# Attention's q, k and v products as pairs of 64-row matmuls with two partial sums each

## The chip, the cores and the metric

The kernel runs on one core of one Trainium2 chip. The metric is the device time of one execution in microseconds (us). A core has the engines TensorE (PE, with its weight loads shown apart as PEld), VectorE (DVE), ScalarE (ACT) and GpSimd (POOL), and a queue on SyncE (SP) that issues all DMA transfers of this kernel in order.

## The reference, cut to what matters

```python
S, D, H, F = 2048, 576, 32, 4608             # Dh = 18, float32 throughout
def reference(A_x, A_wqkv, A_wo, B_x, B_w_gate, B_w_up, B_w_down):
    x = A_x
    xn = layernorm(x)
    q, k, v = heads(xn @ A_wqkv)              # [2048, 576] x [576, 1728]
    s = concat(softmax(q @ k.T * Dh**-0.5) @ v) @ A_wo
    g = silu((gelu(xn @ B_w_gate) * (xn @ B_w_up)) @ B_w_down)
    return x + s * g
```

Every float32 product is built from parts that TensorE's faster float32 format holds exactly: each operand is split into a high part (rounded to that format) and a low part (the rest), and high x high, low x high and high x low are added up.

## The kernel before, in words

The kernel has three stages. A prologue normalises x, transposes it and makes q, k and v. A long middle runs the gate, up and down products of the feed-forward network on TensorE between the attention's score, exponential and value work. An epilogue projects the attention output and multiplies it with the gate. The change touches the prologue alone.

**Blocks and products.** The prologue works on four blocks of 512 tokens (`NB`). `load_x` loads four x tiles of 128 tokens, `norm` computes their statistics on VectorE (`bn_stats`, `bn_aggr`, a few tiny steps) and normalises them, and `transposes` transposes them on TensorE into five PSUM banks; four banks hold the first 512 of the 576 columns, and the fifth holds the last 64 twice, since `norm` copies columns 512 to 576 once more behind the row. `split_t` makes the high part (ACT) and the low part (VectorE) of each bank: `xth`, `xtl`, and one tile `xtr` whose rows 0 to 63 are high and 64 to 127 low. `store_xt` writes them to DRAM (`xhs`) for the feed-forward stage.

For each block, `project` makes nine products of 128 q or k columns by 512 tokens (in the order `ORDER`), and `values_of` eight products of 128 tokens by 288 v columns. `mm_terms` (L174) issues each as 14 matmuls over all 128 rows into one PSUM bank `po`: four chunks each of high x high, low x high and high x low, and two for the last 64 rows. After a q/k product ACT copies the high part `t1` out of PSUM (L290), VectorE subtracts for the low part `t2` (L291), and SP stores both in `qk` (L293). After a v product ACT copies it to one of eight `vn` tiles (L300), and SP stores that in `vs` (L301).

**What sets the order.** TensorE's instructions stand as the program writes them; the other queues are ordered by a scheduler, except where `keep_in_program_order` or a dependence added by hand (`after`) says otherwise. The transposes of the next block are written after the nine q/k products and before the eight v products. In the first block the weights come in as well: `load_qk` and `load_wv` load them to the five `rawp` buffers, GpSimd splits the q/k weights (`split_qk`, L106 and L108), ACT and VectorE the v weights and the 64 rest rows (L116, L117). SP also copies eight pieces of zeros to `zq` there (L376).

**PSUM.** The prologue has eight banks: five for transposes (`pt`) and three for products (`po`). `t1` and `t2` have three buffers each.

**Pairs elsewhere.** The gate and up products (L413) and most down products (L465) are already written as pairs: one matmul over rows 0 to 63 and one over rows 64 to 127, each into a bank of its own.

Of the kernel before, what the change touches and what calls it, by code (L numbers as in the profile page):

```python
# [8 lines left out]
F32 = mybir.dt.float32  # L9
F32R = mybir.dt.float32r  # L10
AF = mybir.ActivationFunctionType
ALU = mybir.AluOpType
# [42 lines left out]
def f(ap):  # L55
    return ap.bitcast(F32)
# [13 lines left out]
def kernel(ctx: ExitStack, tc: tile.TileContext, x, wqkv, wo, w_gate, w_up, w_down, out):  # L70
    nc = tc.nc
# [8 lines left out]
    qk = dram.tile([2, 2 * D, S], F32, name="qk")  # L80
    vs = dram.tile([S, H, DH + 1], F32, name="vs")
# [54 lines left out]
    def load_xd(b, key=None):  # L136
# [11 lines left out]
        return xd  # L148


    TERMS = [(0, k, 0) for k in range(KT)] + [(1, k, 0) for k in range(KT)] + [(0, k, 1) for k in range(KT)] \
        + [(0, KT, 2), (1, KT, 2)]

    FIRST_TERMS = sorted(TERMS[:2 * KT], key=lambda t: 2 * t[1] + 3 * t[0]) + TERMS[2 * KT:]


    with tc.tile_pool(name="pro", bufs=1) as pro, tc.tile_pool(name="pps", bufs=1, space=PSUM) as pps:
# [13 lines left out]
            keep(nc.sync.dma_start(raw, wqkv[0:R0, c0:c0 + n].rearrange("(k p) n -> p k n", p=P)))  # L171
            return raw

        def mm_terms(o, w, cols, xt, toks, swap=False, terms=TERMS):  # L174

            for i, (wp, k, xp) in enumerate(terms):
                xx = xt[xp][:, k, toks] if xp < 2 else xt[2][:, toks]
                ww = w[wp][:, k, cols] if k < KT else w[2 + wp]
                st, m = (xx, ww) if swap else (ww, xx)
                nc.tensor.matmul(o, st, m, start=(i == 0), stop=(i == len(terms) - 1))  # L180

        def tmp2(name):
            return pro.tile([P, TB], F32R, name=name, tag=name, bufs=3)

        def split_t(pt, k, xt):

            if k < KT:
                nc.scalar.activation(xt[0][:, k, :], pt, AF.Copy)
                nc.vector.tensor_tensor(xt[1][:, k, :], pt, f(xt[0])[:, k, :], op=ALU.subtract)
            else:  # L190
                nc.scalar.activation(xt[2], pt, AF.Copy)
                nc.vector.tensor_tensor(xt[2][HR:P, :], pt[HR:P], f(xt[2])[HR:P, :], op=ALU.subtract)

        def load_x(b):
            keep = tc.keep_in_program_order if b == 1 else lambda i: i
            xr = []
            for j in range(4):
                xx = pro.tile([P, D + HR], F32, name="xx", bufs=4)
                keep(nc.sync.dma_start(xx[:, 0:D], x[b * TB + j * P:b * TB + (j + 1) * P, :]))
                xr.append(xx)  # L200
            return xr
# [25 lines left out]

        def warm(n):

            o = pps.tile([P, TB], F32, name="po", bufs=3)  # L230
            for i in range(n):
                nc.tensor.transpose(o[:, 0:P], ident, ident)

        def transposes(b, xr):
            xt = XT[b % 2]
            pts = [pps.tile([P, TB], F32, name="pt", bufs=KT + 1) for k in range(KT + 1)]
            for j in range(4):
                if b == 0 and j == 0:
                    warm(46)
                for k in range(KT + 1):  # L240
                    nc.tensor.transpose(pts[k][:, j * P:(j + 1) * P], xr[j][:, k * P:(k + 1) * P], ident)  # L241
            for k in range(KT + 1):
                split_t(pts[k], k, xt)
            return xt

        def store_xt(b, xt):
            keep = tc.keep_in_program_order if b == 0 else lambda i: i
            for i in range(2):
# [1 line left out]
                keep(nc.sync.dma_start(xhs[b][i, R0:D, :], f(xt[2])[HR * i:HR * i + HR, :]))  # L250

        XT = [(pro.tile([P, KT, TB], F32R, name=f"xth{i}"), pro.tile([P, KT, TB], F32R, name=f"xtl{i}"),
               pro.tile([P, TB], F32R, name=f"xtr{i}")) for i in range(2)]
# [15 lines left out]
        def split_qk(t, raw):  # L269
            hi, lo = (pro.tile([P, KT, P], F32R, name=f"q{m}{t}") for m in "hl")  # L270
            first = split(hi, lo, raw)
            put_qk(t, hi, lo)
            return first
# [10 lines left out]
            WV[c] = hi, lo, VR[0][:, cc], VR[1][:, cc]  # L284

        def project(b, t, xt):
            o = pps.tile([P, TB], F32, name="po", bufs=3)
            mm_terms(o, WQK[t], slice(0, P), xt, all_t, terms=FIRST_TERMS if b == 0 and t == ORDER[0] else TERMS)
            hi, lo = tmp2("t1"), tmp2("t2")
            nc.scalar.activation(hi, o, AF.Copy)  # L290
            nc.vector.tensor_tensor(lo, o, f(hi), op=ALU.subtract)  # L291
            for i, a in enumerate((hi, lo)):
                nc.sync.dma_start(qk[i, t * P:(t + 1) * P, b * TB:(b + 1) * TB], f(a))  # L293

        def values_of(b, j, c, xt):
            t = b * 4 + j
            o = pps.tile([P, TB], F32, name="po", bufs=3)
            mm_terms(o[:, 0:D // 2], WV[c], slice(0, D // 2), xt, slice(j * P, (j + 1) * P), True)
            v = VN[2 * j + c]
            nc.scalar.activation(v[:, :, 1:DH + 1], o[:, 0:D // 2].rearrange("p (h d) -> p h d", d=DH), AF.Copy)  # L300
            nc.sync.dma_start(vs[t * P:(t + 1) * P, c * H // 2:(c + 1) * H // 2, :], v)  # L301

        def split_wo(k):
            n = min(P, D - k * P)
# [12 lines left out]
        t = ORDER[0]  # L317
# [21 lines left out]
        lo = nc.gpsimd.tensor_tensor(qlo, raw, f(qhi), op=ALU.subtract)  # L339
# [4 lines left out]
        xt = transposes(0, xr)  # L344
        for c0 in (slice((t + 1) * P, 2 * D), slice(0, t * P)):
            split_av(QR[0][:, c0], QR[1][:, c0], raw_r[:, c0], tc.keep_in_program_order)
        for b in range(NB):
            for n, t in enumerate(ORDER):
                if n == (2 if b == 0 else 0) and b + 1 < NB:
                    xr = load_x(b + 1)  # L350
                if b == 0 and ahead_qk:
                    first = split_qk(*ahead_qk.pop(0))
                    if n < 3:
                        after(first, last)
                    if n + 4 < NQT:
                        ahead_qk.append(load_qk(ORDER[n + 4]))
                if b == 0 and n == 4:
                    raw_r, VR = load_rest(2 * D, D)
                    split_av(VR[0], VR[1], raw_r, tc.keep_in_program_order)
                if b == 0 and n in (5, 6):  # L360
                    raw_v.append(load_wv(n - 5))
                if b == 0 and n in (7, 8):
                    split_wv(n - 7, raw_v[n - 7])
                project(b, t, xt)
                if b == NB - 1 and 2 <= n < NK + 2:
                    store_wo(*parts.pop(0))
                if b == NB - 1 and n < NK:
                    parts.append(split_wo(n))
                if n == 4 and b + 1 < NB:
                    norm(xr, b + 1)  # L370
            store_xt(b, xt)
            nxt = transposes(b + 1, xr) if b + 1 < NB else None
            if b == 1:
                XD = load_xd(0)
                for i in range(TB // HR):
                    nc.sync.dma_start(zq[:, i * HR:(i + 1) * HR], ident[0:HR - MROW, HR:P])  # L376
# [7 lines left out]
            xt = nxt  # L384

    ffn = ctx.enter_context(tc.tile_pool(name="ffn", bufs=1, reuse_waits="tile"))
    ps = ctx.enter_context(tc.tile_pool(name="ps", bufs=1, space=PSUM, reuse_waits="tile"))
# [257 lines left out]
    with tc.tile_pool(name="att", bufs=1, reuse_waits="tile") as att:  # L645
# [183 lines left out]
        for n in range(NU * NA):  # L829
            u, i = divmod(n, NA)  # L830
# [26 lines left out]
    with tc.tile_pool(name="epi", bufs=1, reuse_waits="tile") as epi:  # L857
# [80 lines left out]
        for n in range(NU * NA, ENDS):  # L938
# [31 lines left out]
            else:  # L970
                for i in range(3):
                    b, j = places[done]
# [69 lines left out]
```

## Time and profile before

| | us |
|---|---|
| median of 3 runs | 2548.03 (2547.41 to 2548.9) |
| span of the profiled execution, first to last instruction | 2545.4 |
| median less that span | 2.6 |
| TensorE busy in the span | 2538.4 |
| VectorE, ACT, GpSimd busy | 1950.4, 1555.1, 1320.7 |
| prologue: first feed-forward matmul starts at | 196.2 |

The profile shows one execution. Rows of the timeline give the start from the beginning of the span, the length, the engine, the line of the kernel, the operation, the tiles written and read, the shape, and in brackets how long the engine was idle before and what ended that. The length of a matmul row is its latency; since matmuls overlap, what a matmul costs is the distance between two starts. Of the profiled execution no other time is recorded than its span.

### The profile page before, as it was taken

Reading aid. Unit: us, or ns where it says so; the run is one execution under the profiler, and the core shown is the slowest. Engines: PE = TensorE matmul, PEld = TensorE weight load, DVE = VectorE, ACT = ScalarE, POOL = GpSimd, SP = SyncE. Lnnn points to the kernel's source line nnn. Section 1 sums busy time; section 2 is a strip of 40 time slices with the busy share of each in tenths; the row PEclk is TensorE's granted clock in tenths of the full one; section 3 lists DMA queues with packets and bytes.
Section 4 is the critical chain, followed back from the end, with each engine's and each line's share of the span. In section 5 each row is a group of like instructions: output and inputs, shape, how many; then the busy total and the mean of one; then the engine's idle time right before and its main releaser. Section 6 shows DMA issues by size and latency. Waiting matters only on the chain.

```text
span 2545.4 us, 63167 instructions
## 1 busy us (share of the span) xinstructions
PE 2538.4 (100%) x23974; PEld 2008.4 (79%) x23974; DVE 1950.4 (77%) x3499; ACT 1555.1 (61%) x3050; POOL 1320.7 (52%) x1447
## 2 busy tenths in 40 slices
PE   9999999999999999999999999999999999999999
PEld 8888877777777777777777787777777777787798
DVE  5316988888888888888888888888888888887277
ACT  3223366666677666676666677666676666676612
POOL 2117545555465554445565545554446555455675
PEclk9999999999999999999999999999999999999999
DMA  8876444444465444444455444444446444444483
GB/s 267 269 241 158 100 103 106 100 111 109 107 150 121 104 109 112 113 112 110 111 125 140 116 111 106 105 108 112 109 109 153 115 109 109 108 106 99 114 242 107
DMA packets 398686, 325.51 MB, mean 128 GB/s; under 512 B 117408, under 2 KB 309184, under 8 KB 398384
## 3 DMA queue, kind: packets, MB, share of 16 engines
q1 hardware_dynamic: 398384, 321.47, 49.7%
q8 instruction: 191, 3.13, 0.5%
q14 instruction: 111, 0.91, 0.1%
HBM read 266.63 MB, written 54.70 MB: 126 GB/s over the span
## 4 chain that ended last, share of the span: by engine, by line
PE 98%; ACT 1%; DVE 0%; DMA 0%; SPq 0%; issue 0%; ACTq 0%
PE pg L413 29%; PE py L465 18%; PE acc L764 18%; PE pm L698 9%; PE pe L729 9%; PE po L180 7%; PE pu L413 6%; PE po L902 2%; ACT pT L730 1%; PE pt L241 0%; SPq L665 0%; DMA xx<-in_A_x_dram 0%; DVE bs L209 0%; ACT t L426 0%; DMA KS<-qk 0%
## 5 line engine op out<-in xcount | busy, mean ns | idle before, releaser
L730 ACT ACTIVATE pT<-pe 128x512 f32<-128x512 f32 x2048 | 1153.3, 598 | 368.7 <-PE pm L698 226.3
L699 DVE TENSOR_REDUCE mx<-pm 128x1 f32<-128x512 f32 x2048 | 1249.6, 680 | 151.3 <-PE pm L698 149.0
L413 PE MATMUL pg<-xd,wh 64*128 64x512 f32 x2592 | 928.9, 390 | 0.0
L413 PE MATMUL pu<-xd,wh 64*128 64x512 f32 x2592 | 928.6, 390 | 0.0
L698 PE MATMUL pm<-KS,q 64*128 64x512 f32 x2048 | 779.0, 388 | 0.8 <-DMA KS<-qk 0.5
L729 PE MATMUL pe<-q,KS 64*128 64x512 f32 x2048 | 775.2, 387 | 0.0
L413 PEld LDWEIGHTS pg<-xd,wh 64*128 64x128 f32 x2592 | 476.5, 184 | 115.9 <-POOL wh L106 21.1
L413 PE MATMUL pg<-xd,wl 64*128 64x512 f32 x1296 | 501.6, 387 | 0.0
L413 PE MATMUL pu<-xd,wl 64*128 64x512 f32 x1296 | 501.4, 387 | 0.0
L413 PEld LDWEIGHTS pu<-xd,wh 64*128 64x128 f32 x2592 | 477.0, 184 | 2.0
L764 PE MATMUL acc<-pT,VS 128*32 128x512 f32 x4096 | 452.8, 594 | 0.0
L108 POOL TENSOR_TENSOR wl<-raw,wh 128x384 fp32r<-128x384 f32 x432 | 434.2, 1019 | 13.7
L106 POOL TENSOR_SCALAR hh<-t 128x512 fp32r<-128x512 f32 x128 | 79.1, 618 | 652.0 <-DVE t L440 637.8
L698 PEld LDWEIGHTS pm<-KS,q 64*128 64x128 f32 x2048 | 374.2, 184 | 31.1 <-DVE mx L699 4.3
L729 PEld LDWEIGHTS pe<-q,KS 64*128 64x128 f32 x2048 | 370.9, 184 | 21.9
L465 PE MATMUL py<-dh,hh 64*128 64x288 f32 (+1 forms) x2160 | 360.3, 294 | 0.3
L465 PE MATMUL py<-dl,hh 64*128 64x288 f32 (+1 forms) x2160 | 358.7, 292 | 0.0
L465 PE MATMUL py<-dh,hl 64*128 64x288 f32 (+1 forms) x2160 | 358.3, 292 | 0.0
L764 PEld LDWEIGHTS acc<-pT,VS 128*32 128x32 f32 x4096 | 127.4, 110 | 289.9 <-issue 278.0
L106 POOL TENSOR_SCALAR wh<-raw 128x384 fp32r<-128x384 f32 x432 | 217.2, 515 | 143.7 <-PE pu L413 83.4
L453 DVE TENSOR_TENSOR Y<-py,Y 128x288 f32<-128x288 f32 x544 | 227.1, 452 | 59.8 <-PE py L465 52.7
L413 PEld LDWEIGHTS pg<-xd,wl 64*128 64x128 f32 x1296 | 238.7, 184 | 32.1
(119 smaller groups left out, 3106.7 us busy)
## 6 DMA issues: line engine op xcount, KB each, us to landing
KS<-qk SPq DMA_DIRECT2D x1536, 36.0 KB
raw<-in_B_w_gate_dram SPq DMA_DIRECT2D x144, 288.0 KB
raw<-in_B_w_up_dram SPq DMA_DIRECT2D x144, 288.0 KB
raw<-in_B_w_down_dram SPq DMA_DIRECT2D x67, 576.0 KB
VS<-vs SPq DMA_DIRECT2D x128, 152.0 KB
qk<-t SPq DMA_DIRECT2D x72, 256.0 KB
q<-qk SPq DMA_DIRECT2D x384, 36.0 KB
xx<-in_A_x_dram SPq DMA_DIRECT2D x32, 288.0 KB
```

The source lines that it names most:

```text
L106: first = nc.gpsimd.tensor_scalar(hi, raw, 1.0, 1.0, op0=ALU.mult, op1=ALU.mult)
L108: low_part[:] = [keep(nc.gpsimd.tensor_tensor(lo, raw, f(hi), op=ALU.subtract))]
L180: nc.tensor.matmul(o, st, m, start=(i == 0), stop=(i == len(terms) - 1))
L413: nc.tensor.matmul(o, w[1 + wp][k][rr, c, :], xd[xp][k][rr, c, :], start=(i == 0), stop=(i == len(terms) - 1))
L453: one = kept(nc.vector.tensor_tensor(yy, py, yy, op=ALU.add))
L465: return nc.tensor.matmul(py, hs[g][a][rr, j * P:(j + 1) * P], wd[w][rr, g, 288 * c:288 * c + 288], start=start, stop=stop)
L698: nc.tensor.matmul(pm, QS[u, r][rr, t * P:(t + 1) * P], KS[(u * NA + c) % KB][r][rr, :], start=True, stop=True)
L699: nc.vector.tensor_reduce(MX[u][:, 2 * r + a, t, c:c + 1], pm, axis=AX.X, op=ALU.max)
L729: nc.tensor.matmul(pe, KS[(u * NA + c) % KB][r][rr, t * P:(t + 1) * P], QS[u, r][rr, :], start=True, stop=True)
L730: nc.scalar.activation(PT[u, kt][:, 2 * r + a, :], pe, AF.Exp, scale=SCALE)
L764: nc.tensor.matmul(ACC[u][32 * a:32 * a + 32, :], VS[(u * NA + c) % VB][:, v:v + 32], pt[:, a, :], start=first, stop=last, skip_group_chec ...
L902: nc.tensor.matmul(po, parts_of(b, j)[x_][:, k, :], OW[w][c][k], start=(i == 0), stop=(i == len(OUT) - 1))
```

## The change

Each product is split by the halves of the array. The matmuls over rows 0 to 63 add up in one PSUM bank, those over rows 64 to 127 in another, and the two streams are issued alternately. For the last 64 rows there are now two tiles, `xtr` (high part below, low part above) and `xtq` (the other way round), and products take them in turn, so that one half has 14 matmuls and the other 13; a half with one more is paired with the first matmul of the next product. The product of the two low parts of those rows is left out. When a product's last matmul is issued, ACT copies the first sum to a tile `both`, VectorE adds the second sum, and from there on a q/k product goes on as before (high part, low part, two stores); in a v product the copy and the sum are made in the `vn` tile.

All PSUM tiles of the prologue, the transposes' too, come from one ring of eight banks. `t1` and `t2` have two buffers each in place of three, `vn` five tiles in place of eight, `both` two.

```diff
-    TERMS = [(0, k, 0) for k in range(KT)] + [(1, k, 0) for k in range(KT)] + [(0, k, 1) for k in range(KT)] \
-        + [(0, KT, 2), (1, KT, 2)]
+    TERMS = [(0, k, 0) for k in range(KT)] + [(1, k, 0) for k in range(KT)] + [(0, k, 1) for k in range(KT)]
...
+    REST = [[[(0, KT, 2), (1, KT, 2)], [(0, KT, 2)]], [[(0, KT, 3)], [(0, KT, 3), (1, KT, 3)]]]
...
-        def mm_terms(o, w, cols, xt, toks, swap=False, terms=TERMS):
-
-            for i, (wp, k, xp) in enumerate(terms):
-                xx = xt[xp][:, k, toks] if xp < 2 else xt[2][:, toks]
-                ww = w[wp][:, k, cols] if k < KT else w[2 + wp]
-                st, m = (xx, ww) if swap else (ww, xx)
-                nc.tensor.matmul(o, st, m, start=(i == 0), stop=(i == len(terms) - 1))
+        HALVES = [[], []]
+        PRODUCTS = [0]
+
+        def product(shape, operands, put, terms=TERMS):
+
+            pos = [pps.tile([P, TB], F32, name="po", bufs=8)[:, 0:shape] for _ in range(2)]
+            parity = PRODUCTS[0] % 2
+            PRODUCTS[0] += 1
+            left = [0]
+            for a in range(2):
+                mine = terms + REST[parity][a]
+                left[0] += len(mine)
+                for i, term in enumerate(mine):
+                    def step(a=a, i=i, term=term, n=len(mine)):
+                        st, m = operands(slice(HR * a, HR * a + HR), *term)
+                        nc.tensor.matmul(pos[a], st, m, start=(i == 0), stop=(i == n - 1))
+                        left[0] -= 1
+                        if left[0] == 0:
+                            put(*pos)
+                    HALVES[a].append(step)
+            while all(HALVES):
+                for half in HALVES:
+                    half.pop(0)()
...
-            return pro.tile([P, TB], F32R, name=name, tag=name, bufs=3)
+            return pro.tile([P, TB], F32R, name=name, tag=name, bufs=2)
...
-                nc.scalar.activation(xt[2], pt, AF.Copy)
-                nc.vector.tensor_tensor(xt[2][HR:P, :], pt[HR:P], f(xt[2])[HR:P, :], op=ALU.subtract)
+                for i, (hi, lo) in enumerate((HALF, HALF[::-1])):
+                    nc.scalar.activation(xt[2 + i], pt, AF.Copy)
+                    nc.vector.tensor_tensor(xt[2 + i][lo, :], pt[lo], f(xt[2 + i])[lo, :], op=ALU.subtract)
...
-            pts = [pps.tile([P, TB], F32, name="pt", bufs=KT + 1) for k in range(KT + 1)]
+            pts = [pps.tile([P, TB], F32, name="po", bufs=8) for k in range(KT + 1)]
...
-        VN = [pro.tile([P, H // 2, DH + 1], F32, name=f"vn{i}") for i in range(8)]
+        VN = [pro.tile([P, H // 2, DH + 1], F32, name=f"vn{i}") for i in range(5)]
...
-            hi, lo = tmp2("t1"), tmp2("t2")
-            nc.scalar.activation(hi, o, AF.Copy)
-            nc.vector.tensor_tensor(lo, o, f(hi), op=ALU.subtract)
-            for i, a in enumerate((hi, lo)):
-                nc.sync.dma_start(qk[i, t * P:(t + 1) * P, b * TB:(b + 1) * TB], f(a))
+            def put(o, o2):
+                both = pro.tile([P, TB], F32, name="both", bufs=2)
+                nc.scalar.activation(both, o, AF.Copy)
+                nc.vector.tensor_tensor(both, both, o2, op=ALU.add)
+                hi, lo = tmp2("t1"), tmp2("t2")
+                nc.scalar.activation(hi, both, AF.Copy)
+                nc.vector.tensor_tensor(lo, both, f(hi), op=ALU.subtract)
+                for i, a in enumerate((hi, lo)):
+                    nc.sync.dma_start(qk[i, t * P:(t + 1) * P, b * TB:(b + 1) * TB], f(a))
...
-            nc.scalar.activation(v[:, :, 1:DH + 1], o[:, 0:D // 2].rearrange("p (h d) -> p h d", d=DH), AF.Copy)
-            nc.sync.dma_start(vs[t * P:(t + 1) * P, c * H // 2:(c + 1) * H // 2, :], v)
+            def put(o, o2):
+                vv = v[:, :, 1:DH + 1]
+                nc.scalar.activation(vv, o.rearrange("p (h d) -> p h d", d=DH), AF.Copy)
+                nc.vector.tensor_tensor(vv, vv, o2.rearrange("p (h d) -> p h d", d=DH), op=ALU.add)
+                nc.sync.dma_start(vs[t * P:(t + 1) * P, c * H // 2:(c + 1) * H // 2, :], v)
```

More of the change, by code (lines that the diff above doesn't have):

```diff
@@ L172, in load_rows, with last_steps, x_part, w_part @@
             return raw
-        def mm_terms(o, w, cols, xt, toks, swap=False, terms=TERMS):
-            for i, (wp, k, xp) in enumerate(terms):
-                xx = xt[xp][:, k, toks] if xp < 2 else xt[2][:, toks]
-                ww = w[wp][:, k, cols] if k < KT else w[2 + wp]
-                st, m = (xx, ww) if swap else (ww, xx)
-                nc.tensor.matmul(o, st, m, start=(i == 0), stop=(i == len(terms) - 1))
+        HALVES = [[], []]
[19 more added lines that the diff above has]
+                    half.pop(0)()
+        def last_steps():
+            for half in HALVES:
+                while half:
+                    half.pop(0)()
+        def x_part(xt, rr, k, xp, toks):
+            return xt[xp][rr, k, toks] if xp < 2 else xt[xp][rr, toks]
+        def w_part(w, rr, k, wp, cols):
+            return w[wp][rr, k, cols] if k < KT else w[2 + wp][rr]
         def tmp2(name):
-            return pro.tile([P, TB], F32R, name=name, tag=name, bufs=3)
+            return pro.tile([P, TB], F32R, name=name, tag=name, bufs=2)
+        HALF = slice(0, HR), slice(HR, P)
         def split_t(pt, k, xt):
@@ L228, in warm @@
         def warm(n):
-            o = pps.tile([P, TB], F32, name="po", bufs=3)
+            o = pps.tile([P, TB], F32, name="po", bufs=8)
             for i in range(n):
@@ L252 @@
         XT = [(pro.tile([P, KT, TB], F32R, name=f"xth{i}"), pro.tile([P, KT, TB], F32R, name=f"xtl{i}"),
-               pro.tile([P, TB], F32R, name=f"xtr{i}")) for i in range(2)]
-        VN = [pro.tile([P, H // 2, DH + 1], F32, name=f"vn{i}") for i in range(8)]
+               pro.tile([P, TB], F32R, name=f"xtr{i}"), pro.tile([P, TB], F32R, name=f"xtq{i}")) for i in range(2)]
+        VN = [pro.tile([P, H // 2, DH + 1], F32, name=f"vn{i}") for i in range(5)]
         eps = pro.tile([P, 1], F32, name="eps")
@@ L286, in project, with operands @@
         def project(b, t, xt):
[L287 to L293 removed]
+            def operands(rr, wp, k, xp):
+                return w_part(WQK[t], rr, k, wp, slice(0, P)), x_part(xt, rr, k, xp, all_t)
+            def put(o, o2):
[7 more added lines that the diff above has]
+                    nc.sync.dma_start(qk[i, t * P:(t + 1) * P, b * TB:(b + 1) * TB], f(a))
+            product(TB, operands, put, FIRST_TERMS if b == 0 and t == ORDER[0] else TERMS)
         def values_of(b, j, c, xt):
             t = b * 4 + j
[L297 to L301 removed]
+            v = VN[(2 * t + c) % len(VN)]
+            def operands(rr, wp, k, xp):
+                return x_part(xt, rr, k, xp, slice(j * P, (j + 1) * P)), w_part(WV[c], rr, k, wp, slice(0, D // 2))
+            def put(o, o2):
[3 more added lines that the diff above has]
+                nc.sync.dma_start(vs[t * P:(t + 1) * P, c * H // 2:(c + 1) * H // 2, :], v)
+            product(D // 2, operands, put)
         def split_wo(k):
@@ L384 @@
             xt = nxt
+        last_steps()
     ffn = ctx.enter_context(tc.tile_pool(name="ffn", bufs=1, reuse_waits="tile"))
```

## The prediction

> **What bounds the kernel now.** I read the busy times and the chain of waits first, then the stretches of time, then the order of each queue in the first 60 us.
>
> ```profile
> PE 2538.4 (100%) x23974; PEld 2008.4 (79%) x23974; DVE 1950.4 (77%) x3499; ACT 1555.1 (61%) x3050; POOL 1320.7 (52%) x1447
> PE 98%; ACT 1%; DVE 0%; DMA 0%; SPq 0%; issue 0%; ACTq 0%
> ...
> 0.00:50.00 50.00, 47.97 (x258) 40.96 (x259) 32.90 (x76) 19.44 (x41) 18.31 (x25) 1.00 0.84 248
> 50.00:100.00 50.00, 50.00 (x287) 44.22 (x286) 16.41 (x35) 12.71 (x30) 8.74 (x6) 1.00 0.90 288
> ```
>
> TensorE is busy all of the 2545.4 us span and carries 98% of the chain, so whatever TensorE saves or waits in the prologue moves the end by as much. In the two stretches (columns: length, then busy PE, PEld, DVE, ACT, POOL, the granted clock, DMA share, GB/s) VectorE has 17 us to spare in the first 50 and DMA is at 84 to 90%. After the prologue nothing is edited.
>
> I call the nine q/k products of a token block p0 to p8 and its eight v products v0 to v7.
>
> **What TensorE saves.** Rows of the timeline (start us, length, engine, line):
>
> ```profile
> 15.02 0.70 PE L180 MATMUL po<-xtr,rest 128*128 128x512 f32 x2
> ...
> 62.06 1.09 PE L180 MATMUL po<-xth,qh 128*128 128x512 f32 x4
> ...
> 65.33 0.86 PE L180 MATMUL po<-xth,qh 128*128 128x512 f32 x3
> ...
> 183.05 0.70 PE L180 MATMUL po<-vh,xth 128*128 128x288 f32 x4
> ...
> 184.92 0.70 PE L180 MATMUL po<-vh,xth 128*128 128x288 f32 x4
> ...
> 196.20 0.50 PE L413 MATMUL pg<-xd,wh 64*128 64x512 f32 x1
> ...
> 200.00 0.39 PE L413 MATMUL pg<-xd,wl 64*128 64x512 f32 x1
> ...
> 202.72 0.39 PE L413 MATMUL pg<-xd,wl 64*128 64x512 f32 x1
> ...
> 1008.47 0.29 PE L465 MATMUL py<-dh,hh 64*128 64x288 f32 x2
> ...
> 1010.05 0.29 PE L465 MATMUL py<-dh,hh 64*128 64x288 f32 x2
> ```
>
> The first product's last terms start at 15.02 and the first feed-forward matmul at 196.20; the products in between, and the transposes, are what the change touches. A q/k product of 14 whole matmuls takes 65.33 - 62.06 = 3.27 us, a v product 184.92 - 183.05 = 1.87. Pairs of 64-row matmuls already run elsewhere: 12 pairs of 512 columns from 200.00 to 202.72, 0.2267 us each, and 12 of 288 columns from 1008.47 to 1010.05, 0.1317 each. The product becomes 24 + 3 halves, 13.5 pairs, because the low-times-low part of the 64 rest rows is dropped: 13.5 x 0.2267 = 3.06 and 13.5 x 0.1317 = 1.78. Gain: 36 x 0.21 + 32 x 0.09 = 10.4 us. The Trainium skill (TensorEngine Tiling (Array Packing), When to Use Tiling) gives row tiling for contractions of 64 or fewer; by it only the rest rows would gain, half a whole matmul in each product. That would be 36 x 0.117 + 32 x 0.067 = 6.3 us (an estimate from the same rows) and an end 4.1 us later; the pair rows above decide for 10.4.
>
> **What ACT and VectorE get.**
>
> ```profile
> L290 ACT ACTIVATE t<-po x36: 576/598/601, 15.8 to 181.4; 128x512 fp32r<-128x512 f32 x36
> L291 DVE TENSOR_TENSOR t<-po,t x36: 682/692/693, 16.9 to 182.0; 128x512 fp32r<-128x512 f32 x36
> ...
> L453 DVE TENSOR_TENSOR Y<-py,Y 128x288 f32<-128x288 f32 x544 | 227.1, 452 | 59.8 <-PE py L465 52.7
> ```
>
> Each q/k product adds one ACT copy (0.60) and one VectorE add (0.69), each v product one add (0.45), each block an xtq copy and subtraction (0.60 and 0.69): VectorE +36 x 0.69 + 32 x 0.45 + 4 x 0.69 = 42 us, ACT +24. By totals this fits: copy, add, high part, low part are 2.6 us in a row against 3.06 a product, and the ring lets a product be four behind. The subtraction of two SBUF tiles has no such row; I take 0.69 (the operand from PSUM) and it may be 0.9. What does not fit is the order in the first block, which I walked queue by queue in the built program, with these lengths.
>
> **The first block: where the gain is lost.** Two edits matter beside the pairs: t1 and t2 have two buffers in place of three, and the scheduler now puts two v-weight loads ahead of all q/k stores on SP. The second waits for the GpSimd split of the sixth q/k weight tile, which in the new order ends after three high and two low parts.
>
> ```profile
> 19.20 1.20 POOL L106 TENSOR_SCALAR qh<-rawp 128x512 fp32r<-128x512 f32 x2
> 20.37 2.53 POOL L108 TENSOR_TENSOR ql<-rawp,qh 128x512 fp32r<-128x512 f32 x2
> ...
> 20.24 3.62 SPq L376 DMA_DIRECT2D zq<-ident  x8
> 23.96 1.82 SPq L293 DMA_DIRECT2D qk<-t  x4
> 25.88 2.22 SPq L199 DMA_DIRECT2D xx<-in_A_x_dram  x4
> ...
> 26.41 0.60 ACT L290 ACTIVATE t<-po 128x512 fp32r<-128x512 f32 x1 [3.52 <-DMA qk<-t]
> 29.83 0.60 ACT L290 ACTIVATE t<-po 128x512 fp32r<-128x512 f32 x1 [2.25 <-DMA qk<-t]
> ...
> 31.09 0.81 DVE L209 BATCH_NORM_STATS2 bs<-xx 128x6 f32<-128x288 f32 x2
> ...
> 39.42 2.05 DVE L223 TENSOR_SCALAR xx<-xx,st 128x576 f32<-128x576 f32 x4
> ...
> 41.99 1.42 DVE L117 TENSOR_TENSOR vl<-rawp,vh 128x576 fp32r<-128x576 f32 x2
> ...
> 43.79 0.78 PE L180 MATMUL po<-vh,xth 128*128 128x288 f32 x4
> ```
>
> The split ends at 19.2 + 3 x 0.60 + 2 x 1.26 = 23.5; a load and the eight zq copies (3.62) follow, so the first store leaves at 27.6, not 23.96. Before, ACT waited for that store until 26.41, 2.45 after its issue, and for p1's (issued 24.9) until 29.83, 4.9 after. With two buffers the high part of p2 now waits: 27.6 + 2.45 = 30.1, and that of p3 for p1's store: 28.5 + 4.9 = 33.4. ACT and VectorE are strictly in order, so their queues stand behind: p3's high part 34.0, low part 34.7, the v rest rows 35.6, then the next block's statistics (four tiles at 0.95, two instructions of 0.81 and an aggregate), ahead of p4's add: 39.4, add 40.1. p8 reuses p4's banks. TensorE starts p1 a pair after those last terms, at 15.25, and wants p8 at 15.25 + 7 x 3.06 = 36.7: **3.4 late**.
>
> Then on VectorE: four small steps 0.8 and the normalising 2.05 to 43.0, p4's low part 43.7; ACT copies p5 by 43.9; add 44.6; p5's high part 45.2; two v-weight copies 46.4; p6's copy 47.0. VectorE: the two vl parts behind them to 47.2, p6's add 47.9; ACT p6's high part 48.5, p7's copy 49.1. The transposes of the next block now take ring banks: p5's two, p6's two and p7's first, so the fifth starts at 49.1. They had banks of their own, which is the cover that is gone. Fifteen more follow. v0's lower half takes the bank of the first transpose, whose low part stands behind p7's add (49.8), p7's high and low parts and the second pair of v weights: 53.1. v0 began at 43.79: **9.3 late**, the gain so far included.
>
> ```profile
> 46.66 0.42 SPq L249 DMA_DIRECT2D xhs<-xth  x1
> ...
> 50.76 4.77 SPq L301 DMA_DIRECT2D vs<-vn  x5
> 55.63 0.90 SPq L199 DMA_DIRECT2D xx<-in_A_x_dram  x2
> ...
> 58.88 0.82 DVE L209 BATCH_NORM_STATS2 bs<-xx 128x6 f32<-128x288 f32 x2 [9.50 <-DMA xx<-in_A_x_dram]
> ```
>
> The v adds now share VectorE's queue with statistics that wait for x. Before, VectorE waited 9.50 us for x and nothing was behind it. Now v2's add stands behind the fourth x tile, whose load stands on SP behind p8's store, which reuses the slot of the first xhs store. That slot came free before at about 55.1 (the fifth of the vs rows, whose data were ready by 43.79 + 5 x 1.87 + 0.41 = 53.5), 8.4 after issue at 46.66. Now it is issued at 51.4 with three x loads beside it, 0.88 MB, 3.1 us at 288 GB/s: 62.9. Then two issues, 3.25 for x (55.63 to 58.88), statistics and small steps 1.8, add 0.45: 69.3. v6 needs that bank at 53.1 + 6 x 1.78 = 63.8: **5.5 late** (2.4 if the x loads cost the store nothing). v3's add follows the normalising, 2.9 later; v7 wants it 1.78 later: **1.1**. So block 1 starts at 53.1 + 8 x 1.78 + 6.6 = 73.9, where it was 43.79 + 8 x 1.87 = 58.7: 15.2 late.
>
> **The other blocks.** They regain 27 x 0.21 + 24 x 0.09 = 7.9. Their stores come in time before. The second boundary again has v2's add behind four statistics, the normalising and the new xtq: 0.5 + 2.5 + 1.4 + 3.8 + 0.9 + 1.2 + 2.05 + 0.45 = 12.8 after the transposes, v6 wants it at 10.7: 2.1. At the third, v0 waits for one transposed low part: 1.1. Together 15.2 - 7.9 + 3.2 = **+10.5 us**.
>
> **The sum.** The profiled execution spans 2545.4; the median of the runs is 2548.0, 2.6 more. 2545.4 + 10.5 + 2.6 = **2558.5 us**. About 0.2% (5 us) can be told from no change here.
>
> **Rivals.**
> - *It does what the pairs promise.* If the stores land 4 us earlier than walked, the ring of eight banks covers everything in the first block and only the last blocks' 3.2 remain: 2548.0 - 10.4 + 3.2 = 2541. The decision point is p8: if p4's add ends by 36.7, TensorE does not stop. For it: past the first block no ACT or VectorE instruction of these products waited for a store. Against: in the first block stores were late already with three buffers. Chance 0.08.
> - *Gain and stalls cancel*: the x loads cost the xhs store nothing (-3.1) and p8 starts 3 us sooner: +4 or less, 2546 to 2552. Chance 0.1.
> - *DMA is slower than these rows*: SP's slots and landings each slip by a few us with 84 to 90% busy engines, VectorE's SBUF subtractions take 0.9: +5, 2563 to 2569. Chance 0.2.
> - *TensorE runs slowly after the long stalls.*
>
> ```profile
> 2.00:4.00 2.00, 2.00 (x12) 1.00 0.98 331
> 6.00:8.00 2.00, 2.00 (x21) 1.00 1.13 302
> ```
>
>   The warm-up transposes run 12 in the first stretch and 21 in the later one, though both rows show a granted clock of 1.00: a cold start costs 40% for about 5 us. If the stalls before p8, around the transposes and at v6 each bring that back, 2 us each, of which the VectorE waits hide a part: +2 to +6, 2561 to 2565. The Trainium skill (TensorE: Matmul & The Clock Gate, Part 1) has such a rule, an idle window of about 3.4 us; no run yet shows it after a stall. Chance 0.12.
>
> **How the numbers follow.** My forecast, 2553 to 2563, has 0.5. All but the first two end slower by over 0.2%: 0.82. The cancelling case gives mostly same: 0.09, the first faster: 0.09 with the remainder. Low end: 2550 (the cancelling case's slower half); high end 2569 (the slow DMA case); 0.15 is left outside.
>
> **What would show it.** Right: matmuls of the new product line with 64 rows at 0.227 and 0.132 spacing; gaps of TensorE at about 37, 44 to 52 and 63 to 70 us, ended by the copy and add of the sums; ACT's high part waiting for the qk stores; the first feed-forward matmul near 207, not 196.20. Wrong: TensorE at 50 of 50 us in the first two stretches, or pairs that take 0.233.

## The result and the profile after

The changed kernel takes 2565.96 us (median of 5 runs, 2564.49 to 2568.34), the kernel before 2547.98 in the same session (5 runs, 2547.41 to 2548.9): a ratio of 1.0072, with a 95% interval of 1.0061 to 1.0083. It is 18.0 us slower by the medians and 17.3 by the spans of the profiled executions (2562.7 and 2545.4). The forecast was 10.5 us slower, 2558.5; the time lies in its range (2550 to 2569), above the likeliest case's own 2553 to 2563.

The busy times, the shares of the chain of waits, and the stretches of time (columns: length, busy PE, PEld, DVE, ACT, POOL, granted clock, DMA share, GB/s) of the changed kernel:

```profile
PE 2542.5 (99%) x24858; PEld 2026.0 (79%) x24858; DVE 1991.9 (78%) x3568; ACT 1578.0 (62%) x3090; POOL 1323.5 (52%) x1447
PE 94%; DVE 2%; ACT 1%; DMA 1%; POOL 1%; SPq 1%; issue 0%; ACTq 0%; DVEq 0%; POOLq 0%
```
```profile
0.00:50.00 50.00, 41.54 (x314) 37.68 (x315) 33.62 (x73) 18.68 (x38) 19.31 (x25) 0.95 0.66 195
50.00:100.00 50.00, 47.22 (x454) 40.81 (x453) 27.38 (x54) 18.64 (x39) 8.91 (x6) 0.91 0.92 296
```

TensorE was idle 2.0 us of the first 50 us before and is idle 8.5 now, and it is not full in the second 50 either. Its share of the chain falls from 98 to 94%, and the chain now passes through VectorE, ACT, DMA and SP. VectorE's total grew by 41.5 us (forecast 42), ACT's by 22.9 (forecast 24). The clock is no longer 1.00.

The first block, from the timelines of SP, ACT, VectorE and TensorE:

```profile
27.60 3.12 SPq L331 DMA_DIRECT2D qk<-t  x4
...
30.96 0.63 ACT L328 ACTIVATE t<-both 128x512 fp32r<-128x512 f32 x1 [7.53 <-DMA qk<-t]
34.40 0.63 ACT L328 ACTIVATE t<-both 128x512 fp32r<-128x512 f32 x1 [2.31 <-DMA qk<-t]
...
62.91 1.19 DVE L241 BATCH_NORM_STATS2 bs<-xx 128x6 f32<-128x288 f32 x3 [4.21 <-DMA xx<-in_A_x_dram]
...
68.47 0.45 DVE L345 TENSOR_TENSOR vn<-vn,po 128x288 f32<-128x288 f32 x1
...
40.78 1.19 PE L191 MATMUL po<-xth,qh 64*128 64x512 f32 x7 [2.83 <-DVE both L326]
...
49.53 3.68 PE L273 MATMUL po<-ident,xx 128*128 128x128 f32 x16 [0.82 <-ACT both L325]
...
53.14 1.95 PE L191 MATMUL po<-vh,xth 64*128 64x288 f32 x8
...
65.94 1.32 PE L191 MATMUL po<-vh,xth 64*128 64x288 f32 x7 [2.04 <-DVE vn L345]
...
74.25 1.09 PE L191 MATMUL po<-xth,qh 64*128 64x512 f32 x8
```

The start of block 1 in the kernel before:

```profile
58.80 1.09 PE L180 MATMUL po<-xth,qh 128*128 128x512 f32 x4
```

The first q/k store leaves at 27.60, ACT's high part of p2 waits 7.53 us for it, p8 waits for p4's sum until 40.78, the fifth transpose bank comes at 49.53, v0 at 53.14, VectorE's statistics wait for x until 62.91 with the v sums behind them (v2's starts at 68.47), and block 1 starts at 74.25, where it was 58.80: 15.4 us late.

The other blocks and what follows (timeline of the changed kernel):

```profile
122.04 1.22 PE L191 MATMUL po<-xth,qh 64*128 64x512 f32 x8
...
147.33 1.22 PE L191 MATMUL po<-xth,qh 64*128 64x512 f32 x8
...
196.78 0.78 PE L191 MATMUL po<-vh,xth 64*128 64x288 f32 x8
...
200.38 0.79 PE L191 MATMUL po<-vh,xth 64*128 64x288 f32 x8
...
211.39 0.41 PE L461 MATMUL pg<-xd,wh 64*128 64x512 f32 x1
...
234.04 0.40 PE L513 MATMUL py<-dl,hh 128*128 128x288 f32 x1 [1.60 <-POOL dl L113]
```

The same down matmul in the kernel before:

```profile
216.93 0.30 PE L465 MATMUL py<-dl,hh 128*128 128x288 f32 x1
```

Eight q/k products take 147.33 - 122.04 = 25.29 us without a wait: 3.16 each, and 0.234 for a pair (forecast 0.2267). Two v products take 3.60: 1.80 each, 0.133 a pair (forecast 0.1317). From block 1 (74.25) to the first feed-forward matmul (211.39) it is 137.1 us, where it was 137.4: nearly nothing is regained. The second down matmul (234.04; 216.93 before) is 17.1 us late where the first feed-forward matmul is 15.2 late: 1.9 more are lost behind the prologue.

### The profile page after: what moved, and what is told of

Read it like the earlier page. It is cut to its first block, busy times and chain, and to the rows that moved or that the text cites. A ratio compares the mean times of both kernels' runs of the same rounds, so it can differ in the third digit from the quotient of the medians.

```text
span 2562.7 us, 65119 instructions
## 1 busy us (share of the span) xinstructions
PE 2542.5 (99%) x24858; PEld 2026.0 (79%) x24858; DVE 1991.9 (78%) x3568; ACT 1578.0 (62%) x3090; POOL 1323.5 (52%) x1447
## 4 chain that ended last, share of the span: by engine, by line
PE 94%; DVE 2%; ACT 1%; DMA 1%; POOL 1%; SPq 1%; issue 0%; ACTq 0%; DVEq 0%; POOLq 0%
PE pg L461 28%; PE acc L812 17%; PE py L513 17%; PE pm L746 9%; PE pe L777 9%; PE pu L461 6%; PE po L191 5%; PE po L950 2%; DVE mx L747 1%; ACT pT L778 1%; DMA xx<-in_A_x_dram 1%; DVE xx L255 0%; DVE bs L241 0%; POOL ql L108 0%; PE po L273 0%
```

## The experiments

The table gives what each kernel's trace shows at three places of TensorE, and its median less that of the kernel before in the same session. A trace is one execution, and runs of one of these kernels spread over up to 5.4 us; read the places as such and the verdict from the medians. An edit can also change the order that the scheduler gives to a queue that the edit doesn't name (e7 and e12 below).

| kernel | v0 | block 1 | feed-forward | median less before | ratio, 95% interval |
|---|---|---|---|---|---|
| before | 43.79 | 58.80 | 196.20 | | |
| changed | 53.14 | 74.25 | 211.39 | +18.0 | 1.0072 (1.0061 to 1.0083) |
| e1 | 52.72 | 75.58 | 212.27 | +18.7 | 1.0070 (1.0054 to 1.0087) |
| e2 | 44.04 | 59.13 | 196.55 | +0.4 | 1.0002 (0.9993 to 1.0011) |
| e3 | 44.56 | 59.57 | 196.98 | +0.5 | one run |
| e4 | 52.86 | 69.35 | 204.10 | +8.7 | 1.0038 (1.0023 to 1.0052) |
| e5 | 45.14 | 61.19 | 203.87 | +6.7 | 1.0026 (1.0016 to 1.0036) |
| e6 | 44.08 | 59.17 | 199.74 | +1.6 | 1.0006 (0.9997 to 1.0015) |
| e7 | 51.65 | 66.65 | 206.49 | +11.2 | 1.0045 (1.0031 to 1.0059) |
| e8 | 50.79 | 73.21 | 207.95 | +12.5 | 1.0049 (1.0035 to 1.0063) |
| e9 | 46.80 | 65.10 | 200.68 | +4.4 | 1.0017 (1.0008 to 1.0026) |
| e10 | 48.27 | 64.71 | 199.18 | +3.2 | 1.0014 (1.0005 to 1.0023) |
| e11 | 44.78 | 59.87 | 201.03 | +0.9 | 1.0005 (0.9996 to 1.0014) |
| e12 | 43.64 | 58.41 | 191.79 | -5.6 | one run |

**The price of a pair.** Why 0.234 here and 0.2267 in the feed-forward stage? The obvious difference was the order of the terms: there two pairs in a row stream the same x tile. Three edits tried it.

```diff
 e1, in the changed kernel (the first product keeps its order)
-    TERMS = [(0, k, 0) for k in range(KT)] + [(1, k, 0) for k in range(KT)] + [(0, k, 1) for k in range(KT)]
+    TERMS = [(wp, k, xp) for k in range(KT) for wp, xp in ((0, 0), (1, 0), (0, 1))]
 e2, in the kernel before
+    TERMS = [(wp, k, xp) for k in range(KT) for wp, xp in ((0, 0), (1, 0), (0, 1))] + [(0, KT, 2), (1, KT, 2)]
 e3, in the kernel before, feed-forward stage
-        terms = [(wp, *divmod(c, XG), xp) for c in range(NC) for wp, xp in ((0, 0), (1, 0), (0, 1))]
+        terms = [(wp, *divmod(c, XG), xp) for wp, xp in ((0, 0), (1, 0), (0, 1)) for c in range(NC)]
```

> The changed kernel with its terms ordered by chunk as the feed-forward pairs have them (high x high, low x high, high x low of one chunk, then the next), so that two pairs in a row stream the same x tile; the first product keeps its order. Theory A (a pair is cheap, 0.2267 us, when the streamed operand stays for the next pair): q/k products start 3.06 us apart in place of 3.165, 27 of them outside the first block give 2.8 us, the end is about 2563. Rival B (the price belongs to something else in this stage, not to the order): 3.16 to 3.17 us apart, no change of the time beyond 1 us.

> The kernel before with whole 128-row matmuls, terms ordered by chunk in the same way. Theory A: a whole matmul of 512 columns goes from 0.2333 to 0.2267 us, a q/k product from 3.27 to 3.17, about 3 us faster than before in all. Rival B: 3.27 us, the time of the kernel before within 1 us. Theory C (only pairs gain from the order): the first run gains and this one does not.

> The kernel before with the gate and up pairs of the feed-forward stage in the order that the prologue has: all nine chunks high x high, then low x high, then high x low. Theory A: a pair goes from 0.2267 to 0.234 us; with 27 pairs in each of 144 products that is up to 28 us slower, and the spacing in the timeline shows it. Rival B: pairs stay at 0.2267 and the time within 5 us of before (the first low parts of the weights may be waited for less).

Rows of e3, the feed-forward pairs in the prologue's order:

```profile
200.33 0.39 PE L413 MATMUL pg<-xd,wl 64*128 64x512 f32 x1
...
201.69 0.39 PE L413 MATMUL pg<-xd,wh 64*128 64x512 f32 x1
```

Six pairs from 200.33 to 201.69: 0.2267, as before. Starts of q/k products in e1 (first two rows) and e2:

```profile
122.44 0.52 PE L192 MATMUL po<-xth,qh 64*128 64x512 f32 x2
...
147.73 0.52 PE L192 MATMUL po<-xth,qh 64*128 64x512 f32 x2
...
118.70 0.39 PE L180 MATMUL po<-xth,qh 128*128 128x512 f32 x1
...
121.97 0.39 PE L180 MATMUL po<-xth,qh 128*128 128x512 f32 x1
```

In e1 eight products take 25.29 us, 3.16 each, and in e2 one takes 3.27, both as they were. Theory A fell three times: the order is not it.

```diff
 e12, in the kernel of e8 (below): only the steps of the lower half are issued
+                    if a == 0:
+                        HALVES[a].append(step)
+                    else:
+                        left[0] -= 1
...
```

> The kernel of e8 without the matmuls of the upper half (left out: all products of rows 64 to 127), so that a product is 13 or 14 matmuls of 64 rows on one half of the array with nothing beside them. It prices one half by itself. Theory A (the partner costs nothing, the matmul of 512 columns takes 0.233 in this stage whether whole, paired or alone): 3.04 to 3.27 us from product to product where nothing waits. Theory B (two halves at work slow each other, 0.234 against the 0.2267 of the feed-forward stage): 0.2267 or less for one alone.

```profile
71.03 1.10 PE L191 MATMUL po<-xth,qh 64*128 64x512 f32 x4
...
77.35 0.86 PE L191 MATMUL po<-xth,qh 64*128 64x512 f32 x3
```

Two products, 27 single 64-row matmuls, take 6.32 us: 0.234 each. In this stage 512 columns cost the same as a single 64-row matmul (0.234), as a pair (0.234) and as one 128-row matmul (0.233). So the partner is free, and the pair saves nothing where all 128 rows were in use. What it saves is the half matmul for each product, 13.5 for 14; e12, which has that and hardly a wait, is 5.6 us faster than the kernel before in its one run (4.4 of it by the first feed-forward matmul). It is not e8 less a partner in everything: the scheduler put its first q/k store back ahead of the v-weight loads (22.93 us; 27.84 in e8). The price of a matmul, read where nothing waits, doesn't depend on that. Why the feed-forward stage runs at 0.2267 stays open.

**Only the rest rows.** If only the rest rows gain, they can be paired without the second sum, between two products:

```diff
 e5, in the kernel before: products 0, 2, ... end with a half, products 1, 3, ... begin with one
...
+            elif half == 0:
+                terms = terms + [(1, KT, 2, slice(0, HR))]
+            else:
+                terms = [(1, KT, 3, slice(HR, P))] + terms
...
```

> The kernel before, whole 128-row matmuls for everything but the last 64 rows: of their two matmuls one stays whole, the other becomes 64 rows, and the last one of a product runs as a pair with the first one of the next product, each into its own product's bank (no second sum, no copy, no added order; the second tile holds only a copy of the high part; five vn tiles; the ninth q/k product of a block and the first two of the first block stay as they were). If a pair costs what a whole matmul costs, so that only the rest rows gain: half a whole matmul in 14 q/k products less than all and 32 v products, 30 x 0.117 + 32 x 0.067 = 5.6 us, 2542. Rival (the gain needs 64-row matmuls next to each other, changing between whole and half costs as much as the pair saves): within 1 us of before.

```profile
70.69 0.82 PE L186 MATMUL po<-xtr,rest 128*128 128x512 f32 x2
71.02 0.49 PE L186 MATMUL po<-xtq,rest 64*128 64x512 f32 x1
71.45 1.20 PE L186 MATMUL po<-xth,qh 128*128 128x512 f32 x4
72.49 1.10 PE L186 MATMUL po<-xth,ql 128*128 128x512 f32 x4
```

A miss, on the rival's side and beyond it: 6.7 us slower. From the last whole matmul at 70.69 to 72.49 there are one whole, one pair and four whole ones; six steps of 0.233 would be 1.40, they take 1.80. Going from 128 rows to 64 and back costs 0.40 us, and the pair saves 0.23. (For v products 95.08 to 96.27 in that trace: 1.19 for 0.80, 0.39 lost and 0.13 saved.) With 15 and 16 such places, 15 x 0.17 + 16 x 0.26 = 6.7. The Trainium skill (TensorEngine Tiling (Array Packing), Key Properties) says that changing the tiling mode drains TensorE; these rows agree and price it.

**What the queues cost.** Four edits of the changed kernel, each taking away one link of the walk through the first block.

```diff
 e4: statistics of the block after next behind the last v sum
+                    if b > 1 and j == 0 and h == 0:
+                        no_sync(one, V_ADD[0], "statistics behind the v sums of the block before")
 e7, added to e4: the first product has 14 matmuls in both halves, so the fifth has no step left over
-            parity = PRODUCTS[0] % 2
+            parity = (PRODUCTS[0] + 1) % 2
...
+                mine = terms + (REST[parity][a] if PRODUCTS[0] > 1 else [(0, KT, 2), (1, KT, 2)])
 e8, in the changed kernel: no copy and no second sum
-                nc.scalar.activation(both, o, AF.Copy)
-                nc.vector.tensor_tensor(both, both, o2, op=ALU.add)
...
 e9, added to e4: v weights behind the second product's stores on SP
+                        no_sync(V_LOADS[0], STORES[3], "v weights behind the second product's stores")
```

> The changed kernel, with one order added: the first statistics of the block after next stand on VectorE behind the last v sum of the block before, so no v sum waits for x any more. If the queue is the cause, as predicted: the stalls of v5, v6 and v7 in the first block (2.0 + 4 us together in the trace) and those before block 2 (2.5) go, 7 to 9 us less: 2557 to 2559. Rival (TensorE was held by stores and DMA there, the queue only shows them): the waits move to the stores or to the transposes of the next block and less than 3 us are won.

```profile
63.91 0.67 PE L192 MATMUL po<-vh,xth 64*128 64x288 f32 x6 [0.53 <-DVE vn L348]
```

Of the waits for v sums 0.53 us is left in the first block, and at the second boundary the wait is gone. (One statistics instruction, which the edit doesn't order, still waits for x until 63.05 with sums behind it.) Against their own kernels before, e4 is 9.3 us better than the change. One order on VectorE, in which sums stood behind statistics that wait for a load, was half of the loss, counted with the slow clock that its waits brought (see the rivals below).

> The kernel of e4, and the first product gets 14 matmuls in both halves (the low x low term is back in it), so that the fifth product is complete before the statistics of the next block are written and its sum stands ahead of them on VectorE. If that order holds p8 up: p8 starts at about 37 in place of 40.8; what follows (sums of p5 to p7, transposes, v0) is bound by ACT and VectorE in a row, so only 1 to 3 us of it reach the end: 2553 to 2555. Rival (p8's wait is all that counts in that stretch): 3.5 us less than e4, 2552. Second rival: the normalising comes later and the transposes with it, no gain or a loss of 1 us.

A miss, 2558.5. p8 no longer waits (the transposes start at 41.73), v0 comes 1.2 us and block 1 2.7 us earlier than in e4, as expected. But the trace doesn't show that the place of the sum did this: the scheduler changed SP's order too. The x loads leave at 18.23 (31.02 in e4), the v weights stand behind the first stores as in e9, and the first store leaves 1.8 us earlier than in e4.

```profile
18.23 1.93 SPq L232 DMA_DIRECT2D xx<-in_A_x_dram  x4
...
26.19 3.49 SPq L334 DMA_DIRECT2D qk<-t  x5
```

At the end e7 is 2.5 us slower than e4: between block 1 and the first feed-forward matmul it loses 5.1, with waits in block 1 (0.78 us for a copy of a sum at 89.82, 0.55 for a sum at 90.87) that e4 does not have. The edit also moves which products of the later blocks have a step left over. That this makes the later loss was not tried by itself.

> The changed kernel without the copy and the sum: only the lower half's sum is used, the upper half's is left out of the result. This takes away 42 us of VectorE and 20 of ACT, but neither the two buffers nor the order of loads, stores and statistics. Theory (the order of the queues costs, not the length of the sums): at most a third of the 18 us go, 2559 to 2563. Rival (the sums are what is too long): most of it goes, 2552 or less.

```profile
43.69 1.66 PE L191 MATMUL po<-xth,qh 64*128 64x512 f32 x7 [3.37 <-DVE t L327]
...
68.09 1.33 PE L191 MATMUL po<-vh,xth 64*128 64x288 f32 x7 [5.30 <-ACT vn L342]
```

Without any sum 12.5 of the 18.0 us are still lost, in the same stretches: q/k products wait for the evacuation of earlier ones, which now ends with the low part, and v products for their copy on ACT. The theory held: the length of the sums is under a third of it.

> The kernel of e4 with one more order: the first load of the v weights stands on SP behind the second q/k product's stores, so that its wait for a weight split no longer holds them up. Theory (the late first stores, met by two t1 and t2 buffers, start the row of delays in the first block): the first store leaves at 23 to 24 us in place of 27.6, p8 starts without a wait, v0 at 48 to 50 in place of 52.9, and the end is 3 to 4 us earlier than e4: 2552. Rival (what fixes v0 is the length of the queues of ACT and VectorE and the ring of eight banks, not the stores): v0 at 52 to 53, 2555 to 2556.

```profile
23.09 2.58 SPq L340 DMA_DIRECT2D qk<-t  x4
...
38.28 1.25 PE L198 MATMUL po<-xth,qh 64*128 64x512 f32 x8
...
49.24 0.66 PE L198 MATMUL po<-vh,xth 64*128 64x288 f32 x6 [1.95 <-DVE xtl L227]
```

The first store leaves at 23.09, p8 starts at 38.28 with no wait, v0 begins at 46.80, earlier than the 48 to 50 expected, but goes on only at 49.24, and the time is 4.3 us better than e4's: the theory, in the main. The store held up by two loads was the first link.

**Buffers and places.**

```diff
 e10, added to e9; t1 and t2 get bufs=3
-                both = pro.tile([P, TB], F32, name="both", bufs=2)
+                both = f(lo)
 e6: first block whole, sums in t2 as in e10, statistics as in e4
+            (whole if b == 0 else product)(TB, operands, put, ...)
 e11: first block and the last block's v products whole, tiles as in the change, statistics as in e4
+            (whole if b in (0, NB - 1) else product)(D // 2, operands, put, TERMS)
```

> The kernel of e9 with sums made in the t2 tile, so that t1 and t2 have three buffers each and the tile for the sum none (the copy of a sum now waits for the store of three products before). Theory (two buffers matter only as long as stores leave late): no change beyond 1 us from e9. Rival A (two buffers by themselves cost): the high part of p2 and p3 wait less, 1 to 3 us faster than e9. Rival B (as in e6, a sum that must wait for a store is worse than a high part that must): waits of TensorE at the second boundary, 2 to 5 us slower than e9.

1.2 us less than e9, within the spread of both; no waits at the second boundary. With early stores the third buffer is worth about nothing. That two buffers cost while the stores are late is argued from ACT's waits for stores in the changed kernel; no run has three buffers and late first stores.

> The changed kernel, but the first block's 17 products are whole matmuls without a second sum, sums are made in the t2 tile so that t1 and t2 have three buffers, and statistics stand behind the v sums as in e4. If the loss is all in the first block's queues, its 15 us go and the other blocks' gain stays: 27 x 0.105 + 24 x 0.07 = 4.5 less 0.7 for the transposes and about 1.6 of waits: 2544 to 2547. Rival (the sums cost in every block): the waits of the other blocks stay as they are and the time is 2549 or more.

> Pairs only where the first block's loads and the end of the prologue are not touched: the first block's 17 products and the last block's v products are whole; the others are pairs as in the changed kernel, two buffers for t1, t2 and the sum, statistics behind the v sums; in the first block these six tiles serve as three buffers. By the price of a pair that the trace shows (0.234 and 0.133) 27 x 0.105 + 16 x 0.07 = 4.0 us are to be had, less 0.7 for transposes and 1 for xtq and waits at the boundaries: 2544 to 2547. If waits for stores in the second block come back as in e6: 2547 to 2550.

e6 lies between its two expectations, e11 in the one for waits that come back, and neither can be told from the kernel before. The first block is cured (block 1 at 59.17 and 59.87). What is then lost is lost in block 1, where the stores are late again, as ACT and TensorE of e6 show:

```profile
89.90 0.60 ACT L338 ACTIVATE t<-po 128x512 f32<-128x512 f32 x1 [2.58 <-DMA qk<-t]
...
90.55 0.47 PE L284 MATMUL po<-ident,xx 128*128 128x128 f32 x1 [2.43 <-ACT t L338]
```

In e11 the transposes wait 2.16 us there. Behind these waits the granted clock is 0.50 for 6.7 us in both traces; the stretch of e11, in the columns used above:

```profile
90.90:97.60 6.70, 5.48 (x22) 4.22 (x24) 3.99 (x7) 3.45 (x8) 0.00 (x0) 0.50 0.73 251
```

In that stretch the last sixteen transposes take 3.6 us (e6, 92.42 to 96.03), where they take 1.9 at full clock (e9, 44.90 to 46.79). The executions of e11 sort by it: six have a mean granted clock of 1.000 and take 2547.1 to 2548.5 us, five have 0.999 and take 2549.9 to 2552.4. So part of what these versions lose, and much of their spread, is the clock behind a wait.

Apart from e12, which leaves out half of each product, no version beats the kernel before. By the price of a pair there were 6 us to be had at most, and each version gives them back in one wait or another and in the slow clock behind it.

## Why the prediction was right, point by point

**The first block** was right almost row by row. First store 27.6 (measured 27.60); high part of p2 30.1 (30.96), of p3 33.4 (34.40); p4's sum ends 40.1 (40.7); fifth transpose bank 49.1 (49.53); v0 53.1 (53.14); block 1 73.9 (74.25). e9 and e4 take its two orders away and win about what the walk gave them (4.3 us for stores that it had 3.6 late; 9.3 for waits that it put at 6.6 in the first block and 2.1 at the second boundary). v0's 53.14 is right in part by luck: its first matmul came straight behind sixteen transposes at half clock (49.53 to 53.13), and the wait that the walk had put there, for the first low part, held its other half:

```profile
53.76 0.98 PEld L191 LDWEIGHTS po<-vh,xth 64*128 64x128 f32 x7 [0.34 <-DVE xtl L220]
```

One stall it placed wrong: v5 waited too (2.04 us, for v1's sum behind the same statistics); the eight v products' delay is 74.25 - 53.14 - 8 x 1.80 = 6.7, forecast 6.6, and made up of these waits and of a slow clock.

**What TensorE saves** is the step that failed: 10.4 us were forecast, from pairs of another stage, and 36 x 0.11 + 32 x 0.07 = 6.2 were measured. The prediction named "pairs that take 0.233" as what would make it wrong, and they take 0.234. The Trainium skill's rule (TensorEngine Tiling (Array Packing), When to Use Tiling), that rows are tiled for contractions of 64 or fewer, had been weighed against the pair rows at 6.3 us and set aside; here it was the better price, and e12 shows why. In blocks 1 to 3 this is 27 x 0.10 + 24 x 0.02 = 3.2 us of the 6.8 by which the span missed.

**The other blocks.** The boundary stalls were right in sum: by what block 1, 2 and 3 take over their products and transposes, 2.6, 1.1 and 0.2 (forecast 2.1, 1.1 and none). "Their stores come in time" was wrong: ACT's high part waits 4.19 us for a store at 88.65, though TensorE shows no wait for it there; e6 and e11 do pay for it. (In the forecast's sum 27 x 0.21 + 24 x 0.09 is 7.8, not 7.9; that changes nothing.) Not foreseen: each of the three boundaries takes 2.34 us from transposes to v0 where it took 2.11, 0.7 in all. This goes with the change of tile height that e5 prices: within e6 it is 2.10 us between whole products and 2.34 between pairs.

```profile
41.98 2.34 PE L284 MATMUL po<-ident,xx 128*128 128x128 f32 x20
44.08 0.78 PE L206 MATMUL po<-vh,xth 128*128 128x288 f32 x4
...
139.76 2.40 PE L284 MATMUL po<-ident,xx 128*128 128x128 f32 x20
142.10 0.80 PE L192 MATMUL po<-vh,xth 64*128 64x288 f32 x8
```

**Nothing after the prologue is edited**, the prediction said, and costed it at nothing. It lost 1.9: SP sends the attention's first load at 212.89 behind the last v store, which now waits for a sum, the down weights are asked for at 224.83 where it was 207.82 (17.0 later, 1.8 more than TensorE), and the first down product waits for their split. That the last sum starts this is argued from the rows and stays open: e11, with whole v products at the end, waits less there (0.68 us from the first down matmul to the second, against 2.00), but so do e10 and e7 with sums to the end (0.97 and 0.24).

So the forecast's miss is 3.2 (pairs), 0.7 (transposes), 1.9 (after), and about 1 in the stalls.

**The rivals.** *It does what the pairs promise*: the ring didn't cover the first block, and e12 shows what was promised was smaller. *DMA is slower*: the time is that of this rival, 2563 to 2569, but not its reason; the first block's slots came when the walk had them. So that the range holds the time is in part luck: its upper end came from this rival, and the likeliest case alone ends at 2563. *TensorE runs slowly after long stalls* came true in part. Stretches of the changed kernel with the granted clock:

```profile
42.00:45.30 3.30, 3.30 (x17) 2.41 (x14) 2.80 (x6) 1.77 (x6) 0.00 (x0) 0.50 0.31 121
...
48.90:55.60 6.70, 6.07 (x32) 5.40 (x34) 5.85 (x10) 5.45 (x11) 0.00 (x0) 0.50 1.02 344
...
65.90:69.20 3.30, 3.26 (x26) 3.26 (x28) 1.99 (x8) 0.60 (x2) 0.00 (x0) 0.50 1.03 394
```

After each of the first block's stalls the clock is at half for a stretch of 3.3 us or twice that; between them and up to the feed-forward stage it is 1.00. In the second of these v0 takes 3.3 us in place of 1.8; half a microsecond of that is its wait for the low part, and about 1 us by the rows is clock that reached the end. The slow p8, transposes and v5 stood ahead of waits that were there anyway. No run took the slow clock away by itself, and it goes with the waits: about 13 us at half clock here, 10 in e4's trace, 7 in e9's, none in the kernel before. What e4 and e9 win is the waits and the clock together. The Trainium skill (TensorE: Matmul & The Clock Gate, Part 1) has the half clock after an idle window of about 3.4 us. The length of the stretches agrees; the wait doesn't, as 2.83 us was enough here, and the half clock began 1.2 us after TensorE had gone on (40.78, 42.0).

## What to carry to other kernels

A pair of half-height matmuls is free only where the other half of the array was empty: price it from a single half in the same stage, not from pairs of another, and count the switch between tile heights (0.40 us there and back). When a step is added between a product and its store, ask of each strictly ordered queue what the new step will stand behind; here half the loss was sums queued behind statistics that wait for a load, and a quarter a store queued behind a load that waits for a split, each with the slow clock that follows a wait of TensorE. Such orders cost nothing to state, and stating two of them won 13.6 of the 18 us.

## What the hardware showed that was not expected

The subtraction of two SBUF tiles, costed at 0.69, "may be 0.9", is 0.69 when GpSimd is idle and up to 1.82 when GpSimd is at work (VectorE, then GpSimd, in the changed kernel):

```profile
79.56 0.69 DVE L329 TENSOR_TENSOR t<-both,t 128x512 fp32r<-128x512 f32 x1 [0.70 <-ACT t L328]
...
82.83 1.82 DVE L329 TENSOR_TENSOR t<-both,t 128x512 fp32r<-128x512 f32 x1 [0.70 <-ACT t L328]
...
82.65 1.47 POOL L146 CAST xd<-xd 64x1536 fp32r<-64x1536 f32 x1 [0.64 <-DMA xd<-xhs]
```

The GpSimd cast ends at 84.12, the subtraction half a microsecond behind that. The Trainium skill (SBUF — State Buffer, SBUF: two separate sides) has this: an operation of VectorE with two SBUF inputs and one of GpSimd that reads SBUF take a shared pair of ports one after the other, each for the whole instruction. The trace agrees; the prediction didn't draw on it.

And the same 64-row matmul of 512 columns stands at 0.234 in one stage and at 0.2267 in another of the same kernel, at a granted clock of 1.00 in both; neither the order of the terms (e1 to e3) nor the partner (e12) makes the difference.
